# One activation table set, a pipelined first batch, and Q transposed by the DMA crossbar in a fused Linformer attention and max-out MoE kernel

## The chip, the cores and the metric

The kernel runs on one core of one Trainium2 chip. The metric is the device time of one execution in microseconds; lower is better. A core has TensorE (PE, matrix products, with its weight loads listed as PEld), VectorE (DVE), ScalarE (ACT), GpSimd (POOL) and SyncE (SP). POOL and SP also issue the DMA transfers here.

## The reference

Eight batches of eight heads, 1024 positions, head dimension 64. K and V are projected along the sequence to 64 rows each by E and F, softmax attention runs against these 64 rows, and the result is the input of a max-out feed-forward layer.

```python
k_proj = np.einsum('ks,bhsd->bhkd', E, k)
v_proj = np.einsum('ks,bhsd->bhkd', F, v)
scores = scale * np.matmul(q, k_proj.transpose(0, 1, 3, 2))
attn = np.exp(scores - max); attn = attn / (sum(attn) + 1e-09)
x = np.matmul(attn, v_proj)            # then heads side by side: 8192 x 512
h1 = x @ w1                            # 512 x 1024
h2 = x @ w2
out = np.maximum(h1, h2) @ w_out       # 1024 x 512, float32
```

## The kernel before

All work is in fp16 with fp32 sums. The order on every engine is the order in which the program is written (`manual_schedule`); no planner moves anything. A DMA or an operation waits by semaphore for its data and for its buffer.

`load` (L75) brings K, V and Q from HBM, cast to fp16 on the way, from POOL's queue: partition p holds positions 8p to 8p+7 of every head. `kvq` has two buffers, so a load of batch b+2 waits for the last reader of batch b. Batch 0 is loaded in six halves (K, V, Q of four heads, then of the other four), then come eight pieces of w1 and w2 (`w_sb`), `wo_sb`, the identity matrix, and the later batches in one transfer each. E and F are loaded first and turned by PE (L109) into `eft`.

The attention of a batch is made of steps:

- `step_kv`: K and V times E and F, 16 matmuls, then copies to `kp` (ACT) and twice to `vp` (DVE).
- `step_kpt`: `kp` transposed by PE, four small copies to `kpt`.
- `step_qt(p)`, p = 0 to 3, two heads each: eight PE transposes of Q into PSUM (L168), one DVE copy to `qt_sb` (L175).
- `step_sc(p)`: four score matmuls (L185), then Exp on ACT to `ex_sb` (L193).
- `step_da(p)`: eight matmuls (L204), four for the softmax sum (`ones`) and four for the product with V; then on ACT Ln of the sum (L212) and Exp of its negative (L213), which is its reciprocal; its `finish` multiplies on DVE into `xt_sb` (L216).

Ln and Exp stand in different table sets as the compiler places them: an ACT_TABLE_LOAD goes ahead of each Ln and of the Exp behind it.

`moe_blocks` gives 24 blocks a batch: for each half j of the positions eight "up" blocks (two groups of four matmuls L234 over `w2_sb` and `w1_sb`, a copy `h_sb` on ACT L241, a maximum on DVE L242 to `gt_sb`) and four "down" blocks (eight matmuls L250, a copy `o_sb` on ACT L257, an output DMA on SP L258). The MoE uses four PSUM banks one after the other (tag `mm`, `mm_ps`), all attention steps use two buffers of two banks each (tag `att`, `att_ps`).

Batch 0's attention runs alone, in two halves of the heads. From then on the steps of batch b+1 stand between the MoE blocks of batch b, as `plan` says: the number is the block behind which a step is written. `finish` of a `step_da` is written behind the next block.

Of the kernel before, what the change touches and what calls it, by code (L numbers as in the profile page):

```python
# [15 lines left out]
def kernel(  # L16
# [12 lines left out]
    nc = tc.nc  # L29
# [15 lines left out]
    kvq = ctx.enter_context(tc.tile_pool(name="kvq", bufs=2))  # L45
    proj = ctx.enter_context(tc.tile_pool(name="proj", bufs=2))
    soft = ctx.enter_context(tc.tile_pool(name="soft", bufs=2))
    xpool = ctx.enter_context(tc.tile_pool(name="xpool", bufs=2))
# [8 lines left out]
    def att_banks(dtype=FP32):  # L57
        return ps.tile(
            [128, 2, 512 if dtype == FP32 else 1024], dtype, tag="att", bufs=2, name="att_ps"
        )  # L60

    ctx.enter_context(tc.manual_schedule())


    ef_sb = const.tile([KP, 2, S], FP16)
    nc.gpsimd.dma_start(out=ef_sb[:, 0, :], in_=E)
    nc.gpsimd.dma_start(out=ef_sb[:, 1, :], in_=F)

    def alloc_kvq():
        t = {}  # L70
# [25 lines left out]
    nc.gpsimd.dma_start(out=wo_sb, in_=moe_w_out.rearrange("(r p) f -> p r f", p=128))  # L96

    ident16 = const.tile([128, 128], FP16)
    make_identity(nc, ident16)
    ones16 = const.tile([128, D], FP16)  # L100
    nc.vector.memset(ones16, 1.0)


    eft = const.tile([128, 2, NC, KP], FP16)
    ef_v = ef_sb.rearrange("kp i (p c) -> kp i c p", c=NC)
    eft_ps = att_banks(FP16)
    for i in range(2):
        for c in range(NC):
            nc.tensor.transpose(  # L109
                out=eft_ps[:, i, c * KP : (c + 1) * KP],  # L110
                in_=ef_v[:, i, c, :],
                identity=ident16[:KP, :KP],
            )
        nc.vector.tensor_copy(
            out=eft[:, i, :, :].rearrange("p c k -> p (c k)"), in_=eft_ps[:, i, 0 : NC * KP]
        )


    def new_attn(t):
        t["kp"] = proj.tile([KP, H, D], FP16, tag="kp", name="kp_sb")  # L120
        t["vp"] = proj.tile([128, H, D], FP16, tag="vp", name="vp_sb")
        t["kpt"] = proj.tile([128, H, KP], FP16, tag="kpt", name="kpt_sb")
        t["xt"] = xpool.tile([128, NP2, 2, HALF], FP16, tag="xt", name="xt_sb")
        t["qt"] = {}
        t["ex"] = {}

    def step_kv(t, h0=0, h1=None):
        h1 = H if h1 is None else h1
        n = (h1 - h0) * D
        kv_ps = att_banks()  # L130
        for c in range(NC):
            nc.tensor.matmul(  # L132
                out=kv_ps[0:KP, 0, 0:n], lhsT=eft[:, 0, c, :], rhs=t["k"][:, h0:h1, c, :],
                start=(c == 0), stop=(c == NC - 1),
            )
            nc.tensor.matmul(  # L136
                out=kv_ps[KP:128, 0, 0:n], lhsT=eft[:, 1, c, :], rhs=t["v"][:, h0:h1, c, :],
                start=(c == 0), stop=(c == NC - 1),
            )
        fl = lambda ap: ap.rearrange("p h d -> p (h d)")  # L140
        nc.scalar.copy(out=fl(t["kp"][:, h0:h1, :]), in_=kv_ps[0:KP, 0, 0:n])  # L141
        nc.vector.tensor_copy(out=fl(t["vp"][KP:128, h0:h1, :]), in_=kv_ps[KP:128, 0, 0:n])
        nc.vector.tensor_copy(out=fl(t["vp"][0:KP, h0:h1, :]), in_=kv_ps[KP:128, 0, 0:n])

    def step_kpt(t, p0=0, p1=None):
        p1 = NP2 if p1 is None else p1
        kpt_ps = att_banks(FP16)
        for p in range(p0, p1):
            nc.tensor.transpose(
                out=kpt_ps[:, 0, p * KP : (p + 1) * KP],  # L150
                in_=t["kp"][:, 2 * p : 2 * p + 2, :],
                identity=ident16[:KP, :KP],
            )
        src = kpt_ps[:, 0, 0 : NP2 * KP].rearrange("q (p k) -> q p k", k=KP)
        dst = t["kpt"].rearrange("q (p e) k -> q p e k", e=2)
        for e in range(2):
            for r in range(2):
                eng = nc.scalar.copy if e == 0 else nc.vector.tensor_copy
                eng(
                    out=dst[r * D : (r + 1) * D, p0:p1, e, :],  # L160
                    in_=src[e * D : (e + 1) * D, p0:p1, :],
                )

    def step_qt(t, p):
        qt_ps = att_banks(FP16)
        for e in range(2):
            for i in range(NI):
                nc.tensor.transpose(  # L168
                    out=qt_ps[:, 0, (e * NI + i) * 128 : (e * NI + i + 1) * 128],
                    in_=t["q"][:, 2 * p + e, 2 * i : 2 * i + 2, :],  # L170
                    identity=ident16,
                )
        qt = soft.tile([128, 2, HALF], FP16, tag="qt", name="qt_sb")
        t["qt"][p] = qt
        nc.vector.tensor_copy(out=qt.rearrange("q e n -> q (e n)"), in_=qt_ps[:, 0, :])  # L175

    def step_sc(t, p):
        sc_ps = att_banks()  # L180
        qt = t["qt"].pop(p)
        for o in range(2):
            for e in range(2):
                pos = D * (o ^ e)
                nc.tensor.matmul(  # L185
                    out=sc_ps[pos : pos + KP, e, :],
                    lhsT=t["kpt"][o * D : (o + 1) * D, 2 * p + e, :],
                    rhs=qt[o * D : (o + 1) * D, e, :],
                    start=True, stop=True,
                )  # L190
        ex = soft.tile([128, 2, HALF], FP16, tag="ex", name="ex_sb")
        t["ex"][p] = ex
        nc.scalar.activation(out=ex, in_=sc_ps, func=ACTF.Exp, scale=scale)  # L193

    def step_da(t, p):
        ex = t["ex"].pop(p)
        dn_ps = att_banks()
        at_ps = att_banks()
        for dst, w in ((dn_ps, None), (at_ps, t["vp"])):
            for r in range(2):  # L200
                for e in range(2):
                    o = r ^ e
                    rows = slice(r * KP, (r + 1) * KP)
                    nc.tensor.matmul(  # L204
                        out=dst[e * D : (e + 1) * D, o, :],
                        lhsT=ones16[rows, :] if w is None else w[rows, 2 * p + e, :],
                        rhs=ex[rows, e, :],
                        start=True, stop=True,
                    )
        ld = soft.tile([128, 2, HALF], FP32, tag="ld", name="ld_sb")  # L210
        rec = soft.tile([128, 2, HALF], FP32, tag="rec", name="rec_sb")
        nc.scalar.activation(out=ld, in_=dn_ps, func=ACTF.Ln)  # L212
        nc.scalar.activation(out=rec, in_=ld, func=ACTF.Exp, scale=-1.0)  # L213

        def finish():
            nc.vector.tensor_tensor(  # L216
                out=t["xt"][:, p, :, :], in0=at_ps, in1=rec, op=ALU.mult
            )

        return finish  # L220
# [45 lines left out]

    t = tiles[0]
    new_attn(t)
    hh = H // 2
    fins = []  # L270
# [15 lines left out]

    for b in range(B):
# [7 lines left out]
        for n, block in enumerate(moe_blocks(b, tiles[b])):  # L295
            block()
            if pending is not None:
                pending()
                pending = None
            if nxt is None:  # L300
                continue
            for s in plan.get(n, ()):
                if isinstance(s, tuple):
                    r = s[0](nxt, s[1])
                else:
                    r = s(nxt)
# [33 lines left out]
```

## Time and profile before

| what | value |
|---|---|
| median of three runs | 506.37 us (505.75 to 507.42) |
| the profiled execution | 505.09 us |
| its span on the core | 503.1 us |
| PE busy | 416.8 us, 83% |
| ACT busy | 296.7 us, 59% |
| DVE busy | 162.5 us, 32% |
| ACT_TABLE_LOAD | 65 loads, 1283 ns each |
| granted TensorE clock | 0.998 of full speed |

How to read it: all times of the trace count from the start of the span. A row of a group gives line, engine, operation, the tiles and their sizes, the count, then busy time, the mean of one in ns, and the idle time of the engine ahead of it with what ended it. A row of the timeline or of the chain begins with its start and its length in us. PE matmuls are pipelined and their ends are modelled, so the time that one costs is read from start to start. For a DMA, the time to landing runs from its issue to the last of its completion signals.

### The profile page before, as it was taken

How to read it: one execution, taken by the hardware profiler on the slowest of the kernel's cores; microseconds unless marked ns; L12 is line 12 of the kernel's file. 1: busy time of each engine (PE TensorE's matmuls, PEld its weight loads, DVE VectorE, ACT ScalarE, POOL GpSimd, SP SyncE). 2: the span in 40 equal slices, each digit the busy share in tenths (PEclk: the TensorE clock that was granted, in tenths of full speed). 3: DMA queues.
4: the chain of work that ended last, by engine and by line, in shares of the span. 5: the costliest groups of instructions: out<-in, count | busy, mean ns of one | idle time of the engine just before them, and what ended most of it. 6: DMA issues, size and time to landing. Idle time of an engine off the chain costs nothing.

```text
span 503.1 us, 5945 instructions
## 1 busy us (share of the span) xinstructions
PE 416.8 (83%) x2368; PEld 181.7 (36%) x2368; DVE 162.5 (32%) x231; ACT 296.7 (59%) x380; POOL 31.5 (6%) x44
## 2 busy tenths in 40 slices
PE   0053379888997999888988999889988999799997
PEld 0032124333443344333433344333433344334443
DVE  0023225242514334233524243242524252342231
ACT  1036644788367753887366854876467845866332
POOL 6321000000100010000100010000000000000000
PEclk9999999999999999999999999999999999999999
DMA  8999949233761629152751549152020011102112
GB/s 127 201 201 207 207 79 165 87 45 77 130 126 43 97 77 169 76 78 90 111 120 24 103 96 177 44 83 85 0 85 1 22 63 43 42 1 83 43 42 83
DMA packets 39675, 45.73 MB, mean 91 GB/s; under 512 B 1632, under 2 KB 31328, under 8 KB 39648
## 3 DMA queue, kind: packets, MB, share of 16 engines
q0 software_dynamic: 30432, 28.58, 36.8%
q1 hardware_dynamic: 9216, 16.78, 8.7%
q8 instruction: 18, 0.29, 0.2%
q14 instruction: 9, 0.07, 0.0%
HBM read 57.15 MB, written 16.78 MB: 147 GB/s over the span
## 4 chain that ended last, share of the span: by engine, by line
PE 48%; ACT 28%; issue 11%; DVE 8%; DMA 3%; POOL 1%; ACTq 0%; POOLq 0%
PE mm_ps L234 32%; PE mm_ps L250 8%; ACT L212 8%; ACT ld_sb L212 7%; DVE xt_sb L216 6%; ACT rec_sb L213 5%; DMA w_sb<-in_moe_w_dram 3%; PE att_ps L168 3%; ACT h_sb L241 3%; PE att_ps L132 3%; ACT ex_sb L193 2%; ACT o_sb L257 2%; ACT L213 1%; PE att_ps L185 1%; DVE gt_sb L242 1%
## 5 line engine op out<-in xcount | busy, mean ns | idle before, releaser
L234 PE MATMUL mm_ps<-xt_sb,w_sb 128*128 128x512 f16 x1024 | 238.1, 382 | 4.6 <-DVE xt_sb L216 4.0
L234 PEld LDWEIGHTS <-w_sb 128*128 128x128 f16 x1024 | 95.7, 98 | 126.4 <-issue 24.2
L242 DVE TENSOR_TENSOR gt_sb<-mm_ps,h_sb 128x512 f16<-128x512 f32 x128 | 88.4, 691 | 159.8 <-PE mm_ps L234 100.0
L241 ACT COPY h_sb<-mm_ps 128x512 f32<-128x512 f32 x128 | 74.8, 584 | 91.0 <-PE mm_ps L234 91.0
L250 PE MATMUL mm_ps<-wo_sb,gt_sb 128*128 128x512 f16 x512 | 118.0, 379 | 8.5 <-DVE gt_sb L242 5.5
L216 DVE TENSOR_TENSOR xt_sb<-att_ps,rec_sb 128x1024 f16<-128x1024 f32 x32 | 39.1, 1221 | 121.9 <-ACT rec_sb L213 121.9
L250 PEld LDWEIGHTS <-gt_sb 128*128 128x128 f16 x512 | 48.0, 98 | 73.5 <-issue 12.3
L257 ACT COPY o_sb<-mm_ps 128x512 f32<-128x512 f32 x64 | 35.9, 584 | 46.7 <-PE mm_ps L250 46.7
L193 ACT ACTIVATE ex_sb<-att_ps 128x1024 f16<-128x1024 f32 x32 | 32.9, 1027 | 14.9 <-PE att_ps L185 14.9
L213 ACT ACT_TABLE_LOAD x32 | 41.1, 1283 | 0.6
L212 ACT ACT_TABLE_LOAD x32 | 41.1, 1283 | 0.6
L168 PE MATMUL att_ps<-ident,q_sb 128*128 128x128 f16 x256 | 21.1, 229 | 22.9 <-DVE xt_sb L216 9.7
L213 ACT ACTIVATE rec_sb<-ld_sb 128x1024 f32<-128x1024 f32 x32 | 33.8, 1057 | 0.4
L212 ACT ACTIVATE ld_sb<-att_ps 128x1024 f32<-128x1024 f32 x32 | 32.8, 1024 | 0.4
L168 PEld LDWEIGHTS <-q_sb 128*128 128x128 f16 x256 | 18.2, 102 | 33.5 <-issue 28.4
L141 ACT CAST kp_sb<-att_ps 64x512 f16<-64x512 f32 (+1 forms) x9 | 4.8, 530 | 42.9 <-PE att_ps L136 42.9
L185 PE MATMUL att_ps<-qt_sb,kpt_sb 64*64 64x512 f16 x128 | 14.0, 426 | 12.5 <-DVE qt_sb L175 8.2
L175 DVE COPY qt_sb<-att_ps 128x1024 f16<-128x1024 f16 x32 | 21.9, 684 | 6.1 <-PE att_ps L168 6.1
L109 PE MATMUL att_ps<-ident,ef_sb 64*128 64x64 f16 x16 | 1.3, 241 | 26.1 <-POOL ident masks.py:199 25.6
L132 PE MATMUL att_ps<-k_sb,eft 128*64 128x512 f16 (+1 forms) x72 | 17.4, 390 | 1.3 <-ACT ld_sb L212 1.3
L76 POOL DMA_DIRECT2D q_sb<-in_q_dram x9 | 7.7, 855 | 163.3 <-PE att_ps L168 162.8
L204 PE MATMUL att_ps<-ex_sb,ones 64*64 64x512 f16 x128 | 14.0, 427 | 4.5 <-ACT ex_sb L193 4.5
(29 smaller groups left out, 114.4 us busy)
## 6 DMA issues: line engine op xcount, KB each, us to landing
out_dram<-o_sb SPq DMA_DIRECT2D x64, 256.0 KB, 2.0
k_sb<-in_k_dram POOLq DMA_DIRECT2D x7, 1024.0 KB, 9.3
v_sb<-in_v_dram POOLq DMA_DIRECT2D x7, 1024.0 KB, 14.0
q_sb<-in_q_dram POOLq DMA_DIRECT2D x7, 1024.0 KB, 9.4
w_sb<-in_moe_w_dram POOLq DMA_DIRECT2D x8, 256.0 KB, 14.6
k_sb<-in_k_dram POOLq DMA_DIRECT2D x2, 512.0 KB, 10.0
v_sb<-in_v_dram POOLq DMA_DIRECT2D x2, 512.0 KB, 11.8
q_sb<-in_q_dram POOLq DMA_DIRECT2D x2, 512.0 KB, 13.6
```

What stands on the lines that cost most here:

```text
L132: nc.tensor.matmul(out=kv_ps[0:KP, 0, 0:n], lhsT=eft[:, 0, c, :], rhs=t["k"][:, h0:h1, c, :], start=(c == 0), stop=(c == NC - 1),)
L168: nc.tensor.transpose(out=qt_ps[:, 0, (e * NI + i) * 128 : (e * NI + i + 1) * 128], in_=t["q"][:, 2 * p + e, 2 * i : 2 * i + 2, :], identi ...
L175: nc.vector.tensor_copy(out=qt.rearrange("q e n -> q (e n)"), in_=qt_ps[:, 0, :])
L193: nc.scalar.activation(out=ex, in_=sc_ps, func=ACTF.Exp, scale=scale)
L212: nc.scalar.activation(out=ld, in_=dn_ps, func=ACTF.Ln)
L213: nc.scalar.activation(out=rec, in_=ld, func=ACTF.Exp, scale=-1.0)
L216: nc.vector.tensor_tensor(out=t["xt"][:, p, :, :], in0=at_ps, in1=rec, op=ALU.mult)
L234: nc.tensor.matmul(out=h_ps, lhsT=w_sb[:, r, fb * 128 : (fb + 1) * 128], rhs=xt[:, r, j, :], start=(r == 0), stop=(r == NDC - 1),)
L241: nc.scalar.copy(out=h2, in_=banks[0])
L242: nc.vector.tensor_tensor(out=gt[:, fb, :], in0=banks[1], in1=h2, op=ALU.max)
L250: nc.tensor.matmul(out=op_ps, lhsT=gt[:, fb, i * 128 : (i + 1) * 128], rhs=wo_sb[:, fb, :], start=(fb == 0), stop=(fb == NFB - 1),)
L257: nc.scalar.copy(out=o_sb, in_=op_ps)
```

## The change

Four edits are made together.

1. One ACT table set that holds both Exp and Ln is loaded at the start of the program (`LN_EXP_SET`).
2. Every step but the scores and `step_da` takes its PSUM from the MoE's banks (`mm_bank`), so `att` serves scores, sums and products alone; `ex_sb` gets four buffers.
3. The start is rewritten. E and F come in fp32 on SP's queue, the identity is made behind the first two loads, K and V of all heads come ahead of Q, Q comes in four pieces, and w2's pieces ahead of w1's. Batch 0's `step_kv` and `step_kpt` do all heads at once, the score of the next pair stands ahead of the product of this one, and only the half j = 0 of the positions is finished before the MoE (`step_da_half`); the half j = 1 follows behind blocks 0 to 3.
4. Q of batches 1 to 7 is transposed by one DMA from `q_sb` to a `qt_sb` of the whole batch (`step_qt_dma`), issued on SP and written behind block 1. The plan becomes shorter.

```diff
+LN_EXP_SET = 6
...
-    def mm_bank():
-        return ps.tile([128, 512], FP32, tag="mm", bufs=4, name="mm_ps")
...
+    def mm_bank(dtype=FP32):
         return ps.tile(
-            [128, 2, 512 if dtype == FP32 else 1024], dtype, tag="att", bufs=2, name="att_ps"
-        )
+            [128, 512 if dtype == FP32 else 1024], dtype, tag="mm", bufs=4, name="mm_ps"
+        )
...
+    nc.scalar.add_instruction(
+        mybir.InstLoadActFuncSet(
...
+            act_func_set_id=LN_EXP_SET,
...
+    ef_sb = const.tile([KP, 2, S], FP32)
+    nc.sync.dma_start(out=ef_sb[:, 0, :], in_=E)
+    nc.sync.dma_start(out=ef_sb[:, 1, :], in_=F)
...
     for h0 in (0, H // 2):
         load(tiles[0], "k", k, 0, h0, h0 + H // 2)
         load(tiles[0], "v", v, 0, h0, h0 + H // 2)
-        load(tiles[0], "q", q, 0, h0, h0 + H // 2)
+        if h0 == 0:
+            ident = const.tile([128, 128], FP32)
+            make_identity(nc, ident)
+    for h0 in range(0, H, 2):
+        load(tiles[0], "q", q, 0, h0, h0 + 2)
...
-        for w_sb, w in ((w1_sb, moe_w1), (w2_sb, moe_w2)):
+        for w_sb, w in ((w2_sb, moe_w2), (w1_sb, moe_w1)):
...
+    def step_kv(t):
+        kv_ps = mm_bank()
...
+    def step_kpt(t):
+        kpt_ps = mm_bank(FP16)
...
     def step_qt(t, p):
-        qt_ps = att_banks(FP16)
+        qt_ps = mm_bank(FP16)
...
+    def step_qt_dma(t):
+        t["qt"] = qtp.tile([128, H, HALF], FP16, tag="qt", name="qt_sb")
+        nc.sync.dma_start_transpose(
+            out=t["qt"].rearrange("q h (i p) -> q (h i) p", p=128),
+            in_=t["q"].rearrange("p h c d -> p (h c d)"),
+        )
...
+    def step_da_half(t, p, o):
+        ex = t["ex"][p]
+        da_ps = att_banks()
+        for i in range(2):
+            for e in range(2):
+                r = o ^ e
+                rows = slice(r * KP, (r + 1) * KP)
+                nc.tensor.matmul(
+                    out=da_ps[e * D : (e + 1) * D, i, :],
+                    lhsT=t["vp"][rows, 2 * p + e, :] if i else ones16[rows, :],
+                    rhs=ex[rows, e, :],
+                    start=True, stop=True,
+                )
+        ld = soft.tile([128, HALF], FP32, tag="ldh", name="ldh_sb")
+        rec = soft.tile([128, HALF], FP32, tag="rech", name="rech_sb")
+        nc.scalar.activation(out=ld, in_=da_ps[:, 0, :], func=ACTF.Ln)
+        nc.scalar.activation(out=rec, in_=ld, func=ACTF.Exp, scale=-1.0)
+
+        def finish():
+            nc.vector.tensor_tensor(
+                out=t["xt"][:, p, o, :], in0=da_ps[:, 1, :], in1=rec, op=ALU.mult
+            )
...
-    for g in range(2):
-        step_kv(t, g * hh, (g + 1) * hh)
-        step_kpt(t, g * hh // 2, (g + 1) * hh // 2)
-        for p in range(g * hh // 2, (g + 1) * hh // 2):
-            step_qt(t, p)
-            step_sc(t, p)
-            step_da(t, p)()
-
+    step_kv(t)
+    step_kpt(t)
+    step_qt(t, 0)
+    step_sc(t, 0)
+    for p in range(NP2):
+        if p + 1 < NP2:
+            step_qt(t, p + 1)
+            step_sc(t, p + 1)
+        step_da_half(t, p, 0)()
+
+    first = {n: (step_da_half, n, 1) for n in range(NP2)}
     plan = {
-        1: [step_kv], 3: [step_kpt],
-        4: [(step_qt, 0)], 6: [(step_sc, 0)], 7: [(step_qt, 1)], 9: [(step_da, 0)],
-        10: [(step_sc, 1)], 11: [(step_qt, 2)], 13: [(step_da, 1)],
-        14: [(step_sc, 2)], 15: [(step_qt, 3)], 17: [(step_da, 2)],
+        1: [(step_qt_dma,)],
+        4: [(step_kv,)], 6: [(step_kpt,)], 8: [(step_sc, 0)],
+        11: [(step_da, 0)], 12: [(step_sc, 1)],
+        14: [(step_da, 1)], 15: [(step_sc, 2)], 17: [(step_da, 2)],
         18: [(step_sc, 3)], 20: [(step_da, 3)],
     }
...
+            if b == 0 and n in first:
+                s = first[n]
+                pending = s[0](tiles[0], *s[1:])
```

On ACT, beside the MoE of batch 1, around the first `step_da` between two down blocks (`o_sb`), before:

```order
L193 ACTIVATE ex_sb<-att_ps 128x1024
L241 COPY h_sb<-mm_ps 128x512
L257 COPY o_sb<-mm_ps 128x512 x2
L212 ACT_TABLE_LOAD
L212 ACTIVATE ld_sb<-att_ps 128x1024
L213 ACT_TABLE_LOAD
L213 ACTIVATE rec_sb<-ld_sb 128x1024
L257 COPY o_sb<-mm_ps 128x512
L193 ACTIVATE ex_sb<-att_ps 128x1024
```

On ACT at the first `step_da` beside an MoE, now (`rec_sb` is L234 and `ex_sb` L214 here):

```order
L214 ACTIVATE ex_sb<-att_ps 128x1024
L304 COPY o_sb<-mm_ps 128x512 x3
L233 ACTIVATE ld_sb<-att_ps 128x1024
L234 ACTIVATE rec_sb<-ld_sb 128x1024
L288 COPY h_sb<-mm_ps 128x512
L214 ACTIVATE ex_sb<-att_ps 128x1024
L288 COPY h_sb<-mm_ps 128x512 x2
```

The two table loads are gone, and the whole program keeps one; `step_da` stands behind the last down block of the half instead of the second.

On SP, from its start, as a piece of the difference:

```order
-L258 DMA out_dram<-o_sb 128x512 x64
-L335 UNCONDITIONAL_BRANCH
+L383 UNCONDITIONAL_BRANCH
+L80 DMA ef_sb<-in_E_dram 64x1024
+L81 DMA ef_sb<-in_F_dram 64x1024
+L194 DMA_TRANSPOSE qt_sb<-q_sb 128x32x128
+L305 DMA out_dram<-o_sb 128x512 x8
+L194 DMA_TRANSPOSE qt_sb<-q_sb 128x32x128
+L305 DMA out_dram<-o_sb 128x512 x8
```

Seven transposes now stand on SP's queue, each ahead of a batch's eight output DMAs; each waits there for its Q load and for the last reader of its `qt_sb`.

On POOL, the first DMA issues and the identity, before:

```order
L67 DMA ef_sb<-in_F_dram 64x1024
L76 DMA k_sb<-in_k_dram 128x4x512
L76 DMA v_sb<-in_v_dram 128x4x512
L76 DMA q_sb<-in_q_dram 128x4x512
L76 DMA k_sb<-in_k_dram 128x4x512
L76 DMA v_sb<-in_v_dram 128x4x512
L76 DMA q_sb<-in_q_dram 128x4x512
L92 DMA w_sb<-in_moe_w_dram 128x4x256 x8
L96 DMA wo_sb<-in_moe_w_out_dram 128x8x512
masks.py:197 MEMSET ident_108 128x128
```

And now:

```order
L90 DMA k_sb<-in_k_dram 128x4x512
L90 DMA v_sb<-in_v_dram 128x4x512
masks.py:197 MEMSET ident 128x128
masks.py:199 ISA
masks.py:199 AFFINE_SELECT ident<-ident 128x128
L90 DMA k_sb<-in_k_dram 128x4x512
L90 DMA v_sb<-in_v_dram 128x4x512
L90 DMA q_sb<-in_q_dram 128x2x512 x4
L110 DMA w_sb<-in_moe_w_dram 128x4x256 x8
```

The identity moved from behind seventeen issues to behind two, and V's second half from the fifth place among the loads of K, V and Q to the fourth.

More of the change, by code (lines that the diff above doesn't have):

```diff
@@ L47 @@
     soft = ctx.enter_context(tc.tile_pool(name="soft", bufs=2))
+    qtp = ctx.enter_context(tc.tile_pool(name="qtp", bufs=2))
+    stage = ctx.enter_context(tc.tile_pool(name="stage", bufs=4))
     xpool = ctx.enter_context(tc.tile_pool(name="xpool", bufs=2))
@@ L52, with att_banks @@
     ps = ctx.enter_context(tc.tile_pool(name="ps", bufs=1, space=bass.MemoryType.PSUM))
-    def mm_bank():
-        return ps.tile([128, 512], FP32, tag="mm", bufs=4, name="mm_ps")
-    def att_banks(dtype=FP32):
+    def mm_bank(dtype=FP32):
         return ps.tile(
-            [128, 2, 512 if dtype == FP32 else 1024], dtype, tag="att", bufs=2, name="att_ps"
+            [128, 512 if dtype == FP32 else 1024], dtype, tag="mm", bufs=4, name="mm_ps"
         )
+    def att_banks():
+        return ps.tile([128, 2, 512], FP32, tag="att", bufs=2, name="att_ps")
     ctx.enter_context(tc.manual_schedule())
-    ef_sb = const.tile([KP, 2, S], FP16)
-    nc.gpsimd.dma_start(out=ef_sb[:, 0, :], in_=E)
-    nc.gpsimd.dma_start(out=ef_sb[:, 1, :], in_=F)
+    nc.scalar.add_instruction(
+        mybir.InstLoadActFuncSet(
+            name=nc.get_next_instruction_name(),
+            act_func_set_id=LN_EXP_SET,
+            engine=mybir.EngineType.Activation,
+            ins=[],
+            outs=[],
+        )
[3 more added lines that the diff above has]
+    nc.sync.dma_start(out=ef_sb[:, 1, :], in_=F)
     def alloc_kvq():
@@ L96 @@
     nc.gpsimd.dma_start(out=wo_sb, in_=moe_w_out.rearrange("(r p) f -> p r f", p=128))
-    ident16 = const.tile([128, 128], FP16)
-    make_identity(nc, ident16)
     ones16 = const.tile([128, D], FP16)
     nc.vector.memset(ones16, 1.0)
+    ident16 = const.tile([128, 128], FP16)
+    nc.vector.tensor_copy(out=ident16, in_=ident)
     eft = const.tile([128, 2, NC, KP], FP16)
     ef_v = ef_sb.rearrange("kp i (p c) -> kp i c p", c=NC)
-    eft_ps = att_banks(FP16)
     for i in range(2):
+        eft_ps = mm_bank()
         for c in range(NC):
             nc.tensor.transpose(
-                out=eft_ps[:, i, c * KP : (c + 1) * KP],
+                out=eft_ps[:, c * KP : (c + 1) * KP],
                 in_=ef_v[:, i, c, :],
-                identity=ident16[:KP, :KP],
+                identity=ident[:KP, :KP],
             )
-        nc.vector.tensor_copy(
-            out=eft[:, i, :, :].rearrange("p c k -> p (c k)"), in_=eft_ps[:, i, 0 : NC * KP]
-        )
+        eng = nc.scalar.copy if i else nc.vector.tensor_copy
+        eng(out=eft[:, i, :, :].rearrange("p c k -> p (c k)"), in_=eft_ps)
     def new_attn(t):
@@ L123, in new_attn @@
         t["xt"] = xpool.tile([128, NP2, 2, HALF], FP16, tag="xt", name="xt_sb")
-        t["qt"] = {}
         t["ex"] = {}
[L127 to L130, printed above, removed]
+    def step_kv(t):
+        kv_ps = mm_bank()
         for c in range(NC):
[L132 to L139, printed above, removed]
-        fl = lambda ap: ap.rearrange("p h d -> p (h d)")
[L141 to L148, printed above, removed]
+            for i, n in enumerate(("k", "v")):
+                nc.tensor.matmul(
+                    out=kv_ps[i * KP : (i + 1) * KP, :],
+                    lhsT=eft[:, i, c, :],
+                    rhs=t[n][:, :, c, :],
+                    start=(c == 0), stop=(c == NC - 1),
+                )
+        fl = lambda ap: ap.rearrange("p h d -> p (h d)")
+        nc.scalar.copy(out=fl(t["kp"]), in_=kv_ps[0:KP, :])
+        nc.vector.tensor_copy(out=fl(t["vp"][KP:128]), in_=kv_ps[KP:128, :])
+        nc.vector.tensor_copy(out=fl(t["vp"][0:KP]), in_=kv_ps[KP:128, :])
+    def step_kpt(t):
+        kpt_ps = mm_bank(FP16)
+        for p in range(NP2):
             nc.tensor.transpose(
-                out=kpt_ps[:, 0, p * KP : (p + 1) * KP],
+                out=kpt_ps[:, p * KP : (p + 1) * KP],
                 in_=t["kp"][:, 2 * p : 2 * p + 2, :],
@@ L153, in step_kpt @@
             )
-        src = kpt_ps[:, 0, 0 : NP2 * KP].rearrange("q (p k) -> q p k", k=KP)
+        src = kpt_ps[:, 0 : NP2 * KP].rearrange("q (p k) -> q p k", k=KP)
         dst = t["kpt"].rearrange("q (p e) k -> q p e k", e=2)
@@ L159, in step_kpt @@
                 eng(
-                    out=dst[r * D : (r + 1) * D, p0:p1, e, :],
-                    in_=src[e * D : (e + 1) * D, p0:p1, :],
+                    out=dst[r * D : (r + 1) * D, :, e, :],
+                    in_=src[e * D : (e + 1) * D, :, :],
                 )
     def step_qt(t, p):
-        qt_ps = att_banks(FP16)
+        qt_ps = mm_bank(FP16)
         for e in range(2):
@@ L168, in step_qt @@
                 nc.tensor.transpose(
-                    out=qt_ps[:, 0, (e * NI + i) * 128 : (e * NI + i + 1) * 128],
+                    out=qt_ps[:, (e * NI + i) * 128 : (e * NI + i + 1) * 128],
                     in_=t["q"][:, 2 * p + e, 2 * i : 2 * i + 2, :],
@@ L172, in step_qt @@
                 )
-        qt = soft.tile([128, 2, HALF], FP16, tag="qt", name="qt_sb")
-        t["qt"][p] = qt
-        nc.vector.tensor_copy(out=qt.rearrange("q e n -> q (e n)"), in_=qt_ps[:, 0, :])
+        if "qt" not in t:
+            t["qt"] = qtp.tile([128, H, HALF], FP16, tag="qt", name="qt_sb")
+        nc.vector.tensor_copy(
+            out=t["qt"][:, 2 * p : 2 * p + 2, :].rearrange("q e n -> q (e n)"), in_=qt_ps
+        )
+    def step_qt_dma(t):
+        t["qt"] = qtp.tile([128, H, HALF], FP16, tag="qt", name="qt_sb")
+        nc.sync.dma_start_transpose(
+            out=t["qt"].rearrange("q h (i p) -> q (h i) p", p=128),
+            in_=t["q"].rearrange("p h c d -> p (h c d)"),
+        )
     def step_sc(t, p):
         sc_ps = att_banks()
-        qt = t["qt"].pop(p)
         for o in range(2):
@@ L187, in step_sc @@
                     lhsT=t["kpt"][o * D : (o + 1) * D, 2 * p + e, :],
-                    rhs=qt[o * D : (o + 1) * D, e, :],
+                    rhs=t["qt"][o * D : (o + 1) * D, 2 * p + e, :],
                     start=True, stop=True,
                 )
-        ex = soft.tile([128, 2, HALF], FP16, tag="ex", name="ex_sb")
+        ex = stage.tile([128, 2, HALF], FP16, tag="ex", name="ex_sb")
         t["ex"][p] = ex
@@ L217, in finish @@
                 out=t["xt"][:, p, :, :], in0=at_ps, in1=rec, op=ALU.mult
+            )
+        return finish
+    def step_da_half(t, p, o):
[5 more added lines that the diff above has]
+                rows = slice(r * KP, (r + 1) * KP)
+                nc.tensor.matmul(
+                    out=da_ps[e * D : (e + 1) * D, i, :],
+                    lhsT=t["vp"][rows, 2 * p + e, :] if i else ones16[rows, :],
+                    rhs=ex[rows, e, :],
+                    start=True, stop=True,
+                )
+        ld = soft.tile([128, HALF], FP32, tag="ldh", name="ldh_sb")
[5 more added lines that the diff above has]
+                out=t["xt"][:, p, o, :], in0=da_ps[:, 1, :], in1=rec, op=ALU.mult
             )
@@ L268 @@
     new_attn(t)
-    hh = H // 2
-    fins = []
-    for g in range(2):
-        step_kv(t, g * hh, (g + 1) * hh)
-        step_kpt(t, g * hh // 2, (g + 1) * hh // 2)
-        for p in range(g * hh // 2, (g + 1) * hh // 2):
-            step_qt(t, p)
-            step_sc(t, p)
-            step_da(t, p)()
+    step_kv(t)
+    step_kpt(t)
+    step_qt(t, 0)
+    step_sc(t, 0)
+    for p in range(NP2):
+        if p + 1 < NP2:
[3 more added lines that the diff above has]
+    first = {n: (step_da_half, n, 1) for n in range(NP2)}
     plan = {
-        1: [step_kv], 3: [step_kpt],
-        4: [(step_qt, 0)], 6: [(step_sc, 0)], 7: [(step_qt, 1)], 9: [(step_da, 0)],
-        10: [(step_sc, 1)], 11: [(step_qt, 2)], 13: [(step_da, 1)],
-        14: [(step_sc, 2)], 15: [(step_qt, 3)], 17: [(step_da, 2)],
+        1: [(step_qt_dma,)],
+        4: [(step_kv,)], 6: [(step_kpt,)], 8: [(step_sc, 0)],
+        11: [(step_da, 0)], 12: [(step_sc, 1)],
+        14: [(step_da, 1)], 15: [(step_sc, 2)], 17: [(step_da, 2)],
         18: [(step_sc, 3)], 20: [(step_da, 3)],
@@ L302 @@
             for s in plan.get(n, ()):
[L303 to L306, printed above, removed]
+                r = s[0](nxt, *s[1:])
                 if r is not None:
```

## The prediction

> **What bounds the kernel now.** I read the page first (span, engines, the chain of waits), then cut the span into stretches with the busy time of each engine, then asked in one steady batch what TensorE (PE) waits for, and last followed the first 70 us and the loads.
>
> ```profile
> span 503.1 us, 5945 instructions
> ...
> PE 416.8 (83%) x2368; PEld 181.7 (36%) x2368; DVE 162.5 (32%) x231; ACT 296.7 (59%) x380; POOL 31.5 (6%) x44
> ...
> PE 48%; ACT 28%; issue 11%; DVE 8%; DMA 3%; POOL 1%; ACTq 0%; POOLq 0%
> ```
>
> ```profile
> core 0: us, PE busy (x) PEld busy (x) DVE busy (x) ACT busy (x) POOL busy (x), PEclk, DMA share, GB/s
> 0.00:25.60 25.60, 0.01 (x1) 0.14 (x2) 0.11 (x1) 1.28 (x1) 13.25 (x24) 1.00 1.07 165
> 25.60:68.00 42.40, 18.33 (x136) 9.85 (x136) 10.94 (x18) 24.34 (x26) 5.16 (x6) 1.00 1.26 203
> 128.20:183.80 55.60, 50.87 (x295) 21.89 (x296) 20.05 (x28) 36.72 (x47) 2.62 (x3) 1.00 0.48 95
> 461.70:503.10 41.40, 37.82 (x176) 16.93 (x173) 10.32 (x15) 12.91 (x22) 0.00 (x0) 0.98 0.13 51
> ```
>
> There are two limits. From 0 to 68 us PE does little (0.01 of 25.6 us, then 18.3 of 42.4). From 68 us on seven periods of 55.6 us follow, in which PE is busy 50.9, and a last MoE with no attention beside it. In a steady period PE waits only for this:
>
> ```profile
> PE att_ps L168 <- DVE xt_sb L216: 1.4, 1, 1.4
> PE att_ps L168 <- ACT ex_sb L193: 1.4, 1, 1.4
> PE mm_ps L250 <- DVE gt_sb L242: 0.8, 1, 0.8
> PE att_ps L185 <- ACT ld_sb L212: 0.6, 1, 0.6
> PE mm_ps L250 <- ACT h_sb L241: 0.4, 1, 0.4
> PE mm_ps L234 <- DVE xt_sb L216: 0.2, 1, 0.2
> ```
>
> That is 4.8 us, and each wait stands at the end of the chain that ScalarE (ACT) walks in `step_da`: table, Ln, table, Exp, then VectorE's (DVE) multiply.
>
> **The steady period.** The one table set takes the two loads out of each `step_da`:
>
> ```profile
> L241 ACT COPY h_sb<-mm_ps 128x512 f32<-128x512 f32 x128 | 74.8, 584 | 91.0 <-PE mm_ps L234 91.0
> ...
> L193 ACT ACTIVATE ex_sb<-att_ps 128x1024 f16<-128x1024 f32 x32 | 32.9, 1027 | 14.9 <-PE att_ps L185 14.9
> ...
> L212 ACT ACT_TABLE_LOAD x32 | 41.1, 1283 | 0.6
> ...
> L175 DVE COPY qt_sb<-att_ps 128x1024 f16<-128x1024 f16 x32 | 21.9, 684 | 6.1 <-PE att_ps L168 6.1
> ```
>
> A period has eight loads: 8 x 1.283 = 10.3 us leave ACT, 36.7 busy becomes 26.4. That isn't a gain by itself; the gain is what PE waited. Between `step_da` and the next one stand three blocks of 1.73 us, one score and one `step_da` on PE, 6.1 us; ACT then needs three copies (3 x 0.584) and three activations of about 1.03, 4.9 us. ACT is ahead in each round, so I take all 4.8 us. Q's transposes leave PE and the copies of L175 leave DVE. PE's own costs are read from the starts in its order of time (the second column is a modelled duration):
>
> ```profile
> 72.60 0.40 PE L132 MATMUL att_ps<-k_sb,eft 128*64 128x512 f16 x1
> ...
> 74.45 3.63 PE L234 MATMUL mm_ps<-xt_sb,w_sb 128*128 128x512 f16 x16
> 78.01 0.29 PE L149 MATMUL att_ps<-ident,kp_sb 64*128 64x64 f16 x4
> 78.23 1.90 PE L234 MATMUL mm_ps<-xt_sb,w_sb 128*128 128x512 f16 x8
> 79.97 0.61 PE L168 MATMUL att_ps<-ident,q_sb 128*128 128x128 f16 x8
> 80.42 3.62 PE L234 MATMUL mm_ps<-xt_sb,w_sb 128*128 128x512 f16 x16
> ...
> 90.04 0.41 PE L204 MATMUL att_ps<-ex_sb,ones 64*64 64x512 f16 x4
> ...
> 90.60 1.90 PE L250 MATMUL mm_ps<-wo_sb,gt_sb 128*128 128x512 f16 x8
> ```
>
> Eight transposes take 79.97 to 80.42, 0.45 us; four times, 1.8 us. Each foreign group inside the MoE costs another 0.1 us: 16 MoE matmuls between such groups take 74.45 to 78.01, 0.2225 each, and without any 0.2158 (below). Four groups fewer: 0.4 us. Three of the waits leave the transposes' tail bare (0.61 for 0.45), some 0.4 us. Sum: 4.8 + 1.8 + 0.4 + 0.4 = 7.4 us a period, 55.6 to 48.2; seven periods, 51.8 us. `step_kv` and `step_kpt` now take banks of the MoE's four. Walking those banks round the plan, the three copies of `step_kv` (0.58, 0.64, 0.64) end about 0.5 us before the second bank of block 6 is wanted; I cost it at nothing, and at up to 0.5 us a period, 3.5 us, for the upper end.
>
> **The first batch.** Its rows, in the chain of waits, the loads, and the pure MoE at the end:
>
> ```profile
> 28.36 0.21 PE att_ps L136
> ...
> 31.20 1.03 PE att_ps L168 x8
> ...
> 33.09 0.67 PE att_ps L185 x4
> ```
>
> ```profile
> 67.97 4.70 PE mm_ps L234 x13
> ```
>
> ```profile
> 478.80 13.81 PE mm_ps L234 x64
> ```
>
> ```profile
> L76 POOL DMA_DIRECT2D v_sb<-in_v_dram x1: 800/800/800, 5.4 to 5.4; - x1
> ...
> DMA to landing us min/median/max: 14.5/14.5/14.5
> ```
>
> 64 matmuls in 13.81 us are 0.2158 each; 13 at 67.97 take 4.70, so 1.9 us are lost where PE comes out of a thin stretch. V's second half, fifth of the six half loads, lands at 5.4 + 14.5 = 19.9 us. Now it is fourth. K, V and Q halves are equal transfers in one stream, and 19.9 less an estimated 2.5 for one half gives 17.4. E and F come on SP's queue, the identity is made behind two issues and not behind seventeen, so PE's start falls from 25.6 to the arrival of K and V. From there, at the slow pace of these rows: eight K/V pairs of 2 x 0.21 give 20.9; kp's copy, the transposes, kpt's and vp's copies 23.4; the first Q copy (0.68) and scores (0.67) 24.9. Then the two `att` banks set the round: Q copy, scores, Exp 1.03, half a `step_da` and hand-overs, about 3.1 us a pair of heads, so the third half `step_da` runs at 33.5 and the fourth at 34.7; ACT's two half-size activations (the 584 ns of a 128x512) and DVE's multiplies trail it by 3.1 us. The third matmul of the MoE goes at 37.8 where it went at 67.97: 30.2 us saved. Within the first MoE four late half steps come in (half of 90.04 to 90.60, 0.3, and 0.1 each): +1.6 us.
>
> **The crossbar transpose.** SP issues it ahead of the eight output DMAs of a batch. Nothing in the trace is a transpose, so its price is bounded:
>
> ```profile
> q1 hardware_dynamic: 9216, 16.78, 8.7%
> ...
> out_dram<-o_sb SPq DMA_DIRECT2D x64, 256.0 KB, 2.0
> ```
>
> ```profile
> q0 software_dynamic: 4696, 3.89, 128.9%
> ```
>
> ```profile
> L76 POOL DMA_DIRECT2D q_sb<-in_q_dram x1: 873/873/873, 28.1 to 28.1; - x1
> ...
> DMA to landing us min/median/max: 26.5/26.5/26.5
> ```
>
> SP's queue moved 16.78 MB in 8.7% of 503.1 us of 16 engines: 383 GB/s, or 76 ns a packet. One Q tile is 1.05 MB. By bytes it costs 2.7 us; as 4096 pieces of 256 bytes at 76 ns on 16 engines, 19.5 us. A fixed part of at most 2.0 us (an output's landing) comes on top. Neither end is nearer in kind, so I take the geometric middle, 7.3 us, 9.3 with the landing. A gain below 2.7 is excluded by the bytes.
>
> Steady cover: SP is free after the last output of the batch before, 0.7 us into the MoE, and the scores come after nine blocks of 1.73, K/V (72.60 to 74.45, 1.85) and kpt (0.22): 17.8 - 0.7 = 17.1 us. 9.3 fits, and the loads released after block 4 come at 10.5 us, behind it. Behind the waiting transpose on SP stand only outputs that are made after block 8.
>
> In the first MoE it does not fit. Q of batch 1 lands at 28.1 + 26.5 = 54.6 us; the stream is bound by bytes and I leave it there. PE reaches the scores at 37.8 + 69 x 0.2158 + 1.9 + 1.6 + 2.2 (K/V, kpt) = 58.4. From 28 to 47 us POOL's queue books the engines 128.9%, and with K, V and Q of batch 2 and K and V of batch 3 behind it will go on to about 80, so a second stream gets half at best: 2 x 7.3 + 2.0 = 16.6, landing at 71.2. PE waits 12.8 us and restarts slowly (1.9): +14.7. With the bounds: 54.6 + 4.7 - 58.4 = 0.9, and 2 x 19.5 + 2.0 + 54.6 - 58.4 + 1.9 = 39.1. The Trainium skill, DMA: Bandwidth & Descriptors, "Issuing engines are not separate DMA queues", says that DMAs from SP and POOL run on the same 16 engines and interleave; by it the doubling stands, without it the wait would be 54.6 + 9.3 - 58.4 + 1.9 = 7.4 and the time 7.3 us less. No run here shows two such streams side by side yet.
>
> **Sum.** 503.1 - 30.2 + 1.6 - 51.8 + 14.7 = 437.4 us of span. The profiled execution took 505.09 for 503.1, and the median of the runs is 506.37, 3.3 above the span: 440.7. I say 440.
>
> **Rivals.**
> 1. The transpose is hidden anyway, at the price by bytes and beside the loads: the first wait is 0.9 and not 14.7. 440 - 13.8 = 426. For it: DMA shares of 0.48 in the steady stretch leave room. Against: the stream before 54.6 us is full. The Trainium skill, Advanced Engine Details and Errata, "X-Bar Transpose (TRN2)", says that such transposes run like regular DMAs, at an expected 350 to 400 GB/s; an estimate from that is 2.6 to 3.0 us, which would be this case.
> 2. The crossbar becomes the bound and the change is slower. If it takes the 32 blocks of 128x128 one behind the other, each at up to a small transfer's 2.0 us, the transpose takes 64 us, 47 beyond the cover, in each of seven periods: 426 + 7 x 47 = 755. It decides from (506.4 - 426) / 7 = 11.5 us beyond the cover, 28.6 us a transpose, 0.9 us a block. Against: the rows know only transfers spread over 16 engines. The Trainium skill, VectorE: DVE Perf Modes, "The three transpose paths", gives 390 ns on TensorE and 1309 ns by DMA for a 128x128 block and prefers TensorE; 32 x 1.309 = 41.9 us in series would by an estimate make 600.
> 3. Pieces near the upper price: 19.5 + 2.0 is 21.5, 4.4 beyond the cover, and more where the loads after block 4 slow the rest. With 39 in the first batch and 4.4 to 6 in six others: 440 + 24 + 26 to 36, 490 to 500.
> 4. The table loads stay. The order of the changed program holds one, so I give this no more than 1%.
>
> **How the numbers follow.** Forecast (hidden from batch 2 on, a wait of some us in the first): 0.60, its own range 424 to 468 from the two ends of the first wait, 3.5 for the banks and 3 us either way for the start. Rival 1: 0.17. Rival 3: 0.11. Rival 2: 0.11. Rest 0.01. A range of 420 to 480 holds the forecast and rival 1 and leaves out rivals 2 and 3. A measurement here can tell about 0.3% from no change. Faster: 0.60 + 0.17 + 0.11 = 0.88; the same 0.01; slower 0.11.
>
> **What would show it.** ACT: one table load, Ln and Exp still near 1.03 us. PE: first MoE matmuls in a row from about 38 us, periods of 48 us with under 1 us of waits, and one wait at the first scores of batch 1 for the transpose. DMA issues: a transpose of about 9 us in steady batches. I am wrong if the first group of scores waits for the transpose in every batch, if a transpose shows over 17 us, or if the period stays above 50 us with ACT or a bank as releaser.

## The result

The changed kernel takes 452.8 us (451.68 to 453.34) where the kernel before took 506.06: a ratio of 0.8945, 95% interval 0.8913 to 0.8977. The forecast was 440, range 420 to 480. The profiled execution took 451.68 us, its span is 449.9, 12.5 us above the 437.4 of the sum. Two executions of the versions below (435.26 us with the loads held back, 604.29 us in four pieces) ran in a slower state and are left out of their medians.

The page of the changed kernel, its span, its engines and its chain of waits:

```profile
span 449.9 us, 5369 instructions
...
PE 402.1 (89%) x2128; PEld 168.2 (37%) x2128; DVE 143.5 (32%) x203; ACT 215.5 (48%) x322; POOL 31.9 (7%) x44
...
PE 81%; DMA 18%; POOL 1%; issue 0%; ACT 0%; POOLq 0%
```

ACT and DVE, 36% of the chain before, are gone from it. What is left is PE and DMA. Four stretches of the changed kernel, with the columns of the same view of before:

```profile
0.00:38.60 38.60, 18.29 (x103) 9.05 (x104) 8.26 (x15) 11.85 (x17) 18.70 (x29) 1.00 1.21 191
60.20:83.70 23.50, 0.09 (x1) 0.01 (x1) 0.00 (x0) 0.59 (x1) 0.00 (x0) 0.56 1.20 199
84.00:92.00 8.00, 8.00 (x40) 3.04 (x37) 0.00 (x0) 3.33 (x5) 0.88 (x1) 0.83 0.87 112
115.37:163.50 48.13, 48.13 (x261) 19.98 (x260) 17.38 (x24) 26.43 (x39) 2.63 (x3) 1.00 0.64 131
```

The start is over at 38.6 us and not at 68. A steady period takes 48.13 us, in all of which PE is busy. Between them lies one hole, 60.2 to 83.7 us, in which PE does nothing while the DMA engines are full (share 1.20). PE's timeline there, and the chain of waits:

```profile
58.40 1.89 PE L297 MATMUL mm_ps<-wo_sb,gt_sb 128*128 128x512 f16 x8
83.72 0.64 PE L206 MATMUL att_ps<-qt_sb,kpt_sb 64*64 64x512 f16 x4 [23.43 <-DMA qt_sb<-q_sb]
```

```profile
26.52 25.89 DMA q_sb<-in_q_dram
52.41 0.02 issue
52.42 31.16 DMA qt_sb<-q_sb
83.59 0.14 issue
```

The first scores of batch 1 stand on PE behind block 8 and wait for the transpose, which takes 31.2 us from issue to landing. In the later batches it takes 5.7 (the DMA issues of the page, and the packets while the rows of batch 2's transpose move, 117.9 to 121.9 us):

```profile
qt_sb<-q_sb SPq DMA_TRANSPOSE x7, 5.7
```

```profile
DMA packets 4128, 1.05 MB, mean 262 GB/s; under 512 B 4128, under 2 KB 4128, under 8 KB 4128
```

The other six transposes take 5.6 to 5.8 us. Two questions are left: why one transpose of seven takes five times as long, and which part of the change brought what.

### The profile page after: what moved, and what is told of

It reads as the page before. It is cut to its first block, busy times and chain, and to the rows that moved or that the text cites. A ratio compares the mean times of both kernels' runs of the same rounds, so it can differ in the third digit from the quotient of the medians.

```text
span 449.9 us, 5369 instructions
## 1 busy us (share of the span) xinstructions
PE 402.1 (89%) x2128; PEld 168.2 (37%) x2128; DVE 143.5 (32%) x203; ACT 215.5 (48%) x322; POOL 31.9 (7%) x44
## 3 DMA queue, kind: packets, MB, share of 16 engines
q1 hardware_dynamic: 38272, 24.65, 18.6%
## 4 chain that ended last, share of the span: by engine, by line
PE 81%; DMA 18%; POOL 1%; issue 0%; ACT 0%; POOLq 0%
PE mm_ps L281 47%; PE mm_ps L297 25%; DMA qt_sb<-q_sb 7%; DMA q_sb<-in_q_dram 6%; PE att_ps L225 3%; DMA v_sb<-in_v_dram 3%; PE mm_ps L147 2%; DMA w_sb<-in_moe_w_dram 2%; PE att_ps L206 2%; PE mm_ps L161 0%; POOL k_sb L90 0%; POOL v_sb L90 0%; ACT o_sb L304 0%; POOL ident masks.py:199 0%; POOL ident masks.py:197 0%
## 5 line engine op out<-in xcount | busy, mean ns | idle before, releaser
L297 PE MATMUL mm_ps<-wo_sb,gt_sb 128*128 128x512 f16 x512 | 116.7, 382 | 0.0
L214 ACT ACTIVATE ex_sb<-att_ps 128x1024 f16<-128x1024 f32 x32 | 32.9, 1027 | 31.2 <-PE att_ps L206 31.2
L237 DVE TENSOR_TENSOR xt_sb<-att_ps,rec_sb 128x1024 f16<-128x1024 f32 x28 | 34.1, 1217 | 24.4 <-ACT rec_sb L234 24.4
L206 PE MATMUL att_ps<-qt_sb,kpt_sb 64*64 64x512 f16 x128 | 14.3, 435 | 29.1 <-DMA qt_sb<-q_sb 23.4
L234 ACT ACTIVATE rec_sb<-ld_sb 128x1024 f32<-128x1024 f32 x28 | 29.6, 1057 | 0.9
L147 PE MATMUL mm_ps<-k_sb,eft 128*64 128x512 f16 x64 | 17.2, 413 | 6.3 <-DMA k_sb<-in_k_dram 6.3
L90 POOL DMA_DIRECT2D k_sb<-in_k_dram x9 | 7.8, 867 | 200.0 <-PE mm_ps L147 198.0
L206 PEld LDWEIGHTS <-kpt_sb 64*64 64x64 f16 x128 | 4.0, 106 | 41.8 <-issue 37.5
L147 PE MATMUL mm_ps<-v_sb,eft 128*64 128x512 f16 x64 | 17.0, 413 | 1.9 <-DMA v_sb<-in_v_dram 1.9
L154 ACT CAST kp_sb<-mm_ps 64x512 f16<-64x512 f32 x8 | 4.6, 579 | 26.7 <-PE mm_ps L147 26.7
L147 PEld LDWEIGHTS <-eft 128*64 128x64 f16 x128 | 7.3, 116 | 17.4 <-issue 13.1
L155 DVE CAST vp_sb<-mm_ps 64x512 f16<-64x512 f32 x8 | 5.6, 694 | 25.1 <-ACT kp_sb L154 25.1
L225 PE MATMUL att_ps<-ex_sb,vp_sb 64*64 64x512 f16 x112 | 10.8, 376 | 0.0
## 6 DMA issues: line engine op xcount, KB each, us to landing
v_sb<-in_v_dram POOLq DMA_DIRECT2D x2, 512.0 KB, 10.1
```

Source lines behind the costliest of these rows:

```text
L147: nc.tensor.matmul(out=kv_ps[i * KP : (i + 1) * KP, :], lhsT=eft[:, i, c, :], rhs=t[n][:, :, c, :], start=(c == 0), stop=(c == NC - 1),)
L206: nc.tensor.matmul(out=sc_ps[pos : pos + KP, e, :], lhsT=t["kpt"][o * D : (o + 1) * D, 2 * p + e, :], rhs=t["qt"][o * D : (o + 1) * D, 2 * ...
L225: nc.tensor.matmul(out=dst[e * D : (e + 1) * D, o, :], lhsT=ones16[rows, :] if w is None else w[rows, 2 * p + e, :], rhs=ex[rows, e, :], s ...
L237: nc.vector.tensor_tensor(out=t["xt"][:, p, :, :], in0=at_ps, in1=rec, op=ALU.mult)
L297: nc.tensor.matmul(out=op_ps, lhsT=gt[:, fb, i * 128 : (i + 1) * 128], rhs=wo_sb[:, fb, :], start=(fb == 0), stop=(fb == NFB - 1),)
```

## The experiments

**The table set alone.** The kernel before with the load of the one set at its start, and nothing else.

```diff
+    nc.scalar.add_instruction(mybir.InstLoadActFuncSet(..., act_func_set_id=LN_EXP_SET, ...))
```

> The kernel before with one change: the table set with both Exp and Ln is loaded once at the start. Theory (PE's waits in a steady period all end in the chain with the two loads): 65 table loads become one, the four rounds of the first batch lose 2 x 1.283 us each, 10.3 us, and a period loses its 4.8 us of waits and 0.4 us of tails, 7 x 5.2 = 36: about 460 us, periods of 50.4 us. Rival (the waits have another cause, such as the two attention banks, and the loads were hidden): only the first 10 us, 496 us, periods still over 54.

459.1 us, ratio 0.9092 (0.9068 to 0.9115). A stretch of one period:

```profile
120.00:169.90 49.90, 49.90 (x294) 21.74 (x292) 20.00 (x29) 26.54 (x39) 2.62 (x3) 1.00 0.53 106
```

PE is busy throughout; the 4.8 us of waits were the loads' doing, and the two attention banks of the old plan were no limit.

**The whole change without the DMA transpose.** Q of every batch is transposed on PE, four groups in the plan.

```diff
-        1: [(step_qt_dma,)],
-        4: [(step_kv,)], 6: [(step_kpt,)], 8: [(step_sc, 0)],
-        11: [(step_da, 0)], 12: [(step_sc, 1)],
+        4: [(step_kv,)], 6: [(step_kpt,)], 7: [(step_qt, 0)], 8: [(step_sc, 0)],
+        10: [(step_qt, 1)], 11: [(step_da, 0)], 12: [(step_sc, 1)],
...
```

> The changed kernel with Q of every batch transposed on PE (four groups of eight beside the MoE, written behind blocks 7, 10, 13 and 16), no DMA transpose. Theory (the transpose costs one wait of 23 us in the first MoE and saves 2.2 us in each of seven periods): 452.8 - 24.7 + 7 x 2.2 = 443.5 us, periods of 50.3 us, no wait at the first scores. Rival (the wait at the first scores of batch 1 is for Q's load itself, not for the transpose): Q lands at about 52 and the wait is gone as well, so the rival is told by the periods: if they stay at 48.1 because PE's transposes hide, 428 us.

440.2 us, ratio 0.8702 (0.8665 to 0.8739), periods of 49.9 us:

```profile
55.40:105.30 49.90, 49.90 (x293) 21.77 (x292) 19.85 (x28) 26.40 (x39) 2.63 (x3) 1.00 0.81 156
```

So the DMA transpose, as it stands in the changed kernel, costs 12.6 us. It saves 1.8 us in each of seven periods and loses more in one wait. The wait was not for Q's load: Q of batch 1 lands at 53.9 us here and at 52.4 in the changed kernel, and here no matmul waits for it.

**Only batch 1 on PE.** The same plan for the first MoE alone, the DMA for batches 2 to 7.

```diff
-            for s in plan.get(n, ()):
+            for s in (plan_pe if b == 0 else plan).get(n, ()):
```

> The changed kernel with Q of batch 1 alone transposed on PE, Q of batches 2 to 7 by the DMA. Theory: the 23.4 us wait and its slow restart (1.3 us) go, 2.2 us come for the four groups: 452.8 - 24.7 + 2.2 = 430 us; the transpose of batch 2 meets no load and takes 5.7 us. Rival (the first DMA transpose is slow because it is the first, whatever runs beside it): batch 2's transpose takes about 30 us and PE waits some 13 us for it in the second MoE, 443 us.

429.0 us, ratio 0.8491 (0.8471 to 0.8511). Its six transposes, the first of them included:

```profile
DMA to landing us min/median/max: 5.6/5.6/5.7
```

A first transpose isn't slow for being the first.

**The load stream held back.** POOL reads a column of batch 1's `qt_sb` before it issues the loads of batch 2.

```diff
+            if b == 1:
+                hold = const.tile([128, 1], FP16)
+                nc.gpsimd.tensor_copy(out=hold, in_=tiles[1]["qt"][:, 0, 0:1])
             nxt = tiles[b + 1] = alloc_kvq()
```

> The changed kernel with POOL reading one column of the transposed Q of batch 1 before it issues the loads of batch 2, so that the transpose of batch 1 has the DMA engines alone. Theory (the load stream beside it made 5.7 us into 31.2): it lands about 58 us, before PE wants it at 60; no wait, 452.8 - 24.7 = 428 us, and the loads that come later are hidden. Rival 1 (the first transpose is slow by itself): still 25 to 31 us, 450 us. Rival 2 (the loads held back are late for batch 2): a wait at the projection of batch 2 instead, 435 to 450 us.

428.3 us, ratio 0.846 (0.843 to 0.849). The transposes from issue to landing, and all that PE waits for them:

```profile
DMA to landing us min/median/max: 6.7/6.8/18.6
```

```profile
PE att_ps L206 <- DMA qt_sb<-q_sb: 3.2, 2, 2.1
```

The first transpose takes 6.8 us, so the stream beside it was the cause. PE waits 1.2 us for it. The maximum of 18.6 is the second, which now meets the loads that were held back: cover of 17 us hides all of it but 2.1.

**What the stream takes: packets of half the size.** The loads of batches 2 and 3 are cut into halves of the positions. The bytes stay, each packet writes 512 bytes instead of 1024.

```diff
+                if b in (1, 2):
+                    for c0 in (0, NC // 2):
+                        nc.gpsimd.dma_start(out=nxt[n][:, :, c0 : c0 + NC // 2, :], ...)
```

> The changed kernel with the loads of batches 2 and 3, which run beside the transpose of batch 1, cut into halves of the positions: the same bytes in packets of half the size (512 bytes written, 60 ns, for 1024 bytes, 98 ns). Theory (packet for packet: a 256-byte row waits for one packet of the other queue): 256 x (60 + 6) = 17 us and 4 to start, the transpose takes about 22 us in place of 31.2, the wait is 14, 443 us. Rival (the two queues share the engines by time or by bytes, at a fixed share): 31 us and 453 us as before.

444.1 us, ratio 0.8765 (0.8746 to 0.8785). The transpose takes 21.8 us and PE waits 13.5:

```profile
DMA to landing us min/median/max: 21.8/21.8/21.8
```

```profile
PE att_ps L206 <- DMA qt_sb<-q_sb: 13.5, 1, 13.5
```

The packets of the two queues while the transpose's rows move, first in the changed kernel (56.3 to 83.1 us), then here (57.1 to 74.4):

```profile
q0 software_dynamic: 4121, 4.15, 91.0%
q1 hardware_dynamic: 4165, 1.13, 30.3%
```

```profile
q0 software_dynamic: 4191, 2.11, 88.2%
q1 hardware_dynamic: 4140, 1.08, 46.3%
```

The counts are equal to about 1% in both, whatever the packets' size: one 256-byte row of the transpose for one packet of the loads. (Whether single packets alternate or short bursts of equal number, the counts don't tell.) An engine has 256 rows; 26.8 us are 105 ns a pair and 17.3 us are 68 ns a pair. A fixed share of time or bytes would have left the transpose at 31 us.

**Four pieces.** One DMA for each pair of heads, so that the first scores need a quarter.

```diff
+        for p in range(NP2):
+            hs = slice(2 * p, 2 * p + 2)
+            nc.sync.dma_start_transpose(out=t["qt"][:, hs, :]..., in_=t["q"][:, hs, :, :]...)
```

> The changed kernel with each transpose cut into four DMAs, one for each pair of heads, so that the first scores need a quarter. Theory (one transposed 256-byte row is let through for each packet of the load stream, 104 ns for the two, 64 rows an engine in a piece): the pieces of batch 1 land at about 63, 70, 77 and 83 us, the scores want them at 60, 71, 77 and 83: waits of 3 to 5 us in all instead of 23.4, 433 us. Rival (a transpose only gets going when the stream lets up, its start and not its rate is late): the first piece lands near 80 and the wait stays, 450 us.

432.4 us, ratio 0.8542 (0.8523 to 0.8561). The first piece lands 11.3 us after its issue, and one wait of 6.1 us is left (3 to 5 were expected, and the first piece about 1 us earlier); the other three pieces arrive in time:

```profile
PE att_ps L208 <- DMA qt_sb<-q_sb: 6.1, 1, 6.1
```

It is mostly the rate that is slow and little the start: in the changed kernel the first rows move 3.9 us after the issue beside the stream and 1.2 us alone (52.4 to 56.3, 116.7 to 117.9), but the rows then take 26.8 us in place of 4.0.

**The change without the table set.** The compiler then places a load ahead of each Ln and of the Exp behind it again.

```diff
-    nc.scalar.add_instruction(mybir.InstLoadActFuncSet(...))
```

> The changed kernel without the one table set: the compiler again puts a load ahead of each Ln and each Exp behind it. Theory (the loads, not the plan, made PE wait): a round of three blocks takes PE 6.1 us and ACT now 4.9 + 2.57 = 7.4, three rounds a period cost about 4 us, periods of 52 us, and the start is some 8 us later, which the wait for the transpose absorbs: 452.8 + 6 x 4 = 477 us. Rival (the new plan with its banks hides the loads): 453 to 457 us, periods of 48.1.

480.2 us, ratio 0.9486 (0.9457 to 0.9515). A period, and PE's waits in it:

```profile
180.20:232.60 52.40, 49.05 (x261) 20.10 (x261) 17.19 (x24) 36.46 (x47) 2.63 (x3) 1.00 0.58 121
```

```profile
PE mm_ps L272 <- ACT h_sb L279: 1.2, 2, 0.6
PE mm_ps L288 <- DVE gt_sb L280: 0.8, 1, 0.8
PE att_ps L197 <- ACT ld_sb L224: 0.6, 1, 0.6
PE mm_ps L288 <- ACT h_sb L279: 0.6, 1, 0.6
```

The new plan does not hide the loads: the period is 52.4 us, 4.3 longer. The wait for the transpose is down to 3.6 us, since PE comes 16 us later (76.4 and not 60.3) and the transpose takes 27.1 us: the stream of loads lets up before its end.

**The held-back version with another tile width.** `hold` becomes 128 elements wide, of which POOL still writes one.

```diff
-                hold = const.tile([128, 1], FP16)
-                nc.gpsimd.tensor_copy(out=hold, in_=tiles[1]["qt"][:, 0, 0:1])
+                hold = const.tile([128, 128], FP16)
+                nc.gpsimd.tensor_copy(out=hold[:, 0:1], in_=tiles[1]["qt"][:, 0, 0:1])
```

> The kernel that holds back the loads of batch 2, with the small tile that POOL writes made 256 bytes a partition wide instead of 2, so that the tiles behind it keep the place in the partition that they have in the changed kernel modulo 256 bytes. In the version before, all transposes took 6.7 us and more where the changed kernel has 5.7. Theory (the 256-byte rows had lost their alignment): 5.7 us again for the undisturbed transposes, and the run 1 us faster or the same, 427 us. Rival (the chip or the run): 6.8 us as before.

427.85 us, ratio 0.8448 (0.843 to 0.8465): the lowest median of the study, though the narrow tile (428.3) and batch 1 on PE (429.0) lie within 0.3% of it. The transposes, and PE's wait for them:

```profile
DMA to landing us min/median/max: 5.6/5.6/16.7
```

```profile
PE att_ps L206 <- DMA qt_sb<-q_sb: 0.2, 1, 0.2
```

The undisturbed transpose is back at 5.6 us: beside the 2-byte tile it took 1.1 us longer. That alignment to 256 bytes is the reason is argued from the size of the rows; which tile had moved by how much was not tried. The tile is not all that moves this time: in the version without the table set, which has no such tile, the undisturbed transposes take 5.9 to 6.0 us.

## Why the prediction was right, and where it missed

- **The steady period was right.** 7.4 us were forecast; 55.56 became 48.15 (PE's own order of time, batch to batch). The parts can be told apart: the table set alone brings 5.6 (periods of 49.9) where its terms made 5.2, Q off PE another 1.8 where they made 2.2. The banks that `step_kv` and `step_kpt` now share with the MoE cost nothing: the version with PE transposes has the same 49.9 as the old plan with the table set.
- **ACT's loads as such were rightly not counted.** 10.3 us a period left ACT (36.72 to 26.43 busy) and 5.6 came out of the time.
- **The start was 0.8 us off, and that is partly luck.** The fourth matmul of the MoE (the prediction calls it the third) starts at 38.61 where it started at 67.97, 29.4 us earlier instead of 30.2. Two misses offset each other in it. V's second half landed at 15.8 us and not 17.4, and the first scores ended at 23.5 and not 24.9; but a pair of heads then took 4.2 us and not 3.1. The two `att` banks did not set that round: on DVE the copy of the next Q (L187) stands behind the multiply of the half before (L263), ahead of which DVE sits idle 2.95 us for ACT's reciprocal. Between 38.61 and the scores of batch 1 PE took 1.1 us more than the sum said.
- **The price of an undisturbed transpose was set too high, within its bounds.** 9.3 us were taken, from 4.7 to 21.5; 5.7 were measured. The rows take 4.0 us of it, 262 GB/s: between the price by bytes and the geometric middle. So the steady cover of 17.1 us held with room. This case agrees with the 261 GB/s that the Trainium skill, DMA: Bandwidth & Descriptors, "Latency and other measured facts", gives for a transpose with a non-contiguous middle dimension. It does not agree with the 350 to 400 of rival 1, nor with rival 2's 1309 ns for each block in series.
- **The step that failed is the price of the company in the first MoE.** "A second stream gets half at best" was turned into a doubling, 16.6 us; the transpose took 31.2. The engines moved as many packets of one queue as of the other, and a transpose has packets of 256 bytes where the loads have 1024. Alone, a row takes some 16 ns of an engine (4.0 us for 256) and a packet of the loads 78 (800 on 16 engines in the 3.9 us ahead of the first rows); together a pair takes 105. So 4.0 us of rows became 26.8 and not 8.0, and 31.2 with start and landing. By the prediction's own sign, "if a transpose shows over 17 us", this step is wrong.
- **In the sum** that term was a wait of 12.8 us; it measured 23.4. Q landed at 52.4 us and not 54.6, and PE came at 60.3 and not 58.4, which took 4 us off the wait. The restart after it cost 1.4 us and not 1.9 (from start to start, the 24 matmuls of the half's last blocks took 6.46 us where those of batch 2 took 5.28, and the scores 0.57 for 0.34).
- **Two errors offset each other there too, by luck.** With the undisturbed price as measured, 4.0 us of rows and 1.7 around them, the doubling would have made 9.7 us, and the prediction's sum a wait of only 5.9. The price that was too high hid part of what the doubling missed. The upper end of the term, 39.1, covered the wait, but it came from twice the upper price of a transpose, which none here had alone.
- **The sum of the misses** is 23.4 + 1.4 - 14.7 = 10.1, and 0.8 and 1.1 from the start: 12.0 of the 12.5 us.
- **Rivals.** Rival 1 (hidden anyway) fails in the first MoE and holds in the other six. Rivals 2 and 3 are out, the undisturbed transpose being 5.7 us, and rival 4 too: the program keeps one table load. The rule of the Trainium skill, DMA: Bandwidth & Descriptors, "Issuing engines are not separate DMA queues", that DMAs from SP and POOL run on the same engines and interleave is borne out by the equal counts; the doubling that the prediction hung on it is not.
- **What the parts brought.** 506 to 459.1 by the table set, to 440.2 by the new start and plan (a difference of two versions; none takes them back alone), and back to 452.8 by the DMA transpose. The parts depend on the order: taken out of the whole change, the table set is worth 27.4 us and not 46.5, as the wait for the transpose absorbs what the loads cost in the start. With the loads held back the transpose becomes a gain of 12.4 us over PE's, 427.85.

## What to carry to other kernels

Price a transfer of small pieces by what shares its engines, not by its bytes: where the two streams moved packet for packet, its time was its packets on one engine times what a pair took, 256 x 105 ns here. Keeping the other stream away brought back all of the loss (428.3 us); cutting the transfer in four, so that its first use needs a quarter, brought back most of it (432.4). A table load or a copy that leaves an engine is worth only what the waits at the end of its chain show, and that can be read before the change: here 4.8 of 10.3 us. When several edits go in together, undo each alone; a good total hid one part that lost 12.6 us.

## What the runs showed of the hardware that was not expected

- Two DMA queues on the same 16 engines move equal numbers of packets, whatever their size: 4121 to 4165 and 4191 to 4140 in the same time, at 105 and 68 ns a pair.
- The issue of a transpose holds SP's queue, and far longer beside the loads: 4.15 us undisturbed, 20.66 us in the first MoE (least, median and most of the seven, in ns):

```profile
L194 SPq DMA_TRANSPOSE qt_sb<-q_sb x7: 4054/4152/20661, 52.4 to 357.4; - x7
```

- The granted TensorE clock falls in the wait of 23 us, to 0.56 on average over it, and stands at 0.83 in the 8 us behind it. The slow restart is not one price: 1.4 us here, 1.9 behind the 6.1 us wait of the four pieces, 2.9 behind the 13.5 us wait with the small packets (the same matmuls each time).
- Idleness alone doesn't decide that clock: in the first 25.6 us of the kernel before PE did as little and it read 1.00. From 25 to 35 us it read 1.00 in the changed kernel and 0.50 in the version with all of Q on PE, whose PE work is the same there. What decides it no run here shows.
- An undisturbed transpose took 6.7 to 6.8 us with a 2-byte tile allocated in the same program and 5.6 to 5.7 with that tile 256 bytes wide; the cause is not shown.
